# Batch 2's q and k by transposed loads, and six output tiles as half sums, in an attention and feed-forward kernel

## The chip, the cores and the metric

The kernel runs on one core of a Trainium2 chip. The metric is device microseconds of one execution. Before the change the median of three runs is 397.52 us (396.32 to 397.59). Engines are named as in the profile: PE (TensorE), with PEld for its weight loads, DVE (VectorE), ACT (ScalarE), POOL (GpSimd) and SP (SyncE, which here only issues DMAs).

## What is computed

```python
scale = 1.0 / np.sqrt(q.shape[-1])
scores = scale * np.matmul(q, k.transpose(0, 1, 3, 2))
m = np.max(scores, axis=-1, keepdims=True)
e = np.exp(scores - m)
attn = e / (np.sum(e, axis=-1, keepdims=True) + np.exp(-m) + 1e-09)
x = np.matmul(attn, v)                  # 8 batches, 12 heads, 448 tokens, 64 wide
x = x.transpose(0, 2, 1, 3).reshape(3584, 768)
h = x @ w_in                            # w_in 768 x 2048
g = np.maximum(h, 0.0) ** 2
out = g @ w_out                         # w_out 2048 x 768
```

Inputs and outputs are float32; the kernel computes in fp16 with float32 sums.

## The kernel before, in words

**Units.** A batch has 448 tokens and 12 heads; four heads are a *quad*, so a batch has three. Tokens are taken in seven chunks of 64. Scores come out transposed (keys on partitions): for one chunk of keys of a quad, PE writes a pair of PSUM banks (`sp`, two of these pairs) and ACT takes the exponential into fp16 (`exp`, line 245). The sum over keys is made by adding the chunks on DVE (`add_quad`) and by a matmul with ones; ACT makes the reciprocal as exp of minus ln; DVE multiplies it onto the values' product and so makes x (`quad_x`, line 478), transposed, which is what the in-projection wants. The in-projection (`half_in` for batch 0 in half-width tiles, `later_in` for the others) is followed by relu (ACT or DVE), a square on DVE into the ring `gs`, and the output product (`out_piece`, line 536), 384 columns of 128 tokens a tile, 16 blocks of 128 long in the sum. There are 56 such tiles.

**Shapes on PE.** The 128x128 array is used in three shapes. Scores, values and sums use four 64x64 quarters at once. The transposes of q and k use 128 rows by 64 columns. The in-projection of batches 0 and 1 and the first six output tiles use the full array. From batch 2 on (the cycles below) the in-projection runs as two column halves, and an output tile as four 64x64 products per block: the upper and the lower 64 rows of the sum go to two different PSUM banks, and two DVE or ACT instructions put them together (`out_first` scales the one bank into SBUF, `out_second` adds the other).

**How q and k are transposed.** `ON_PE` (line 37) names batches 0, 1 and 2: their q and k are loaded quad by quad with a cast to fp16 (`load_natural_quads`, POOL's queue), PE transposes chunk by chunk into PSUM (`transpose_one`, line 194: 14 matmuls for q or k of a quad), and DVE or ACT copies the result into `qk` (`transposed_copy`, line 201). Batches 3 to 7 go another way. `stage` (line 143, POOL's queue) copies q and k of a batch as fp16 into a buffer in DRAM; `transposed_loads` (line 160, SP's queue) reads it back with three transposing DMAs into `qk`: q, k, and k shifted by one token, since a row of 128 holds two tokens of 64. Even and odd keys then lie in different planes and halves, so a chunk of scores takes eight matmuls of 224 columns instead of four of 448 (`quad_scores`, line 391), and the last chunk's keys are put together by four copies on POOL (`tail_keys`, line 171).

**Order.** Nothing is scheduled by a program at run time: each engine works its own queue in the order in which the code emits. That order is written out in two strings. `ORDER` (line 662) holds everything up to 105.9 us: attention of batches 0 and 1 and most of 2, the in-projection of 0 and 1 and six output tiles. Its steps have one letter and numbers: `t`, `u`, `T`, `U` transposes and their copies, `s` and `e` a chunk of scores and its exponential (numbers up to 23 are batch 0 in half-width pieces; from 24 on seven to a quad), `p`, `b`, `y`, `z`, `n`, `x` values, sums, reciprocal and x of batch 0, `v`, `a`, `S`, `Z`, `M`, `X` the same for later quads, `i`, `r`, `g` and `j`, `k`, `l` in-projection, relu and square, `o`, `O` an output tile's product and its eviction, `d` a load out of the list `LOADS` (line 614). `CYCLE` (line 719) is then run for batches 3 to 7: attention of that batch, in-projection of the batch before, seven output tiles. Its only load step, `d0`, stands near its end and issues all that belongs to the next batch (`following`, line 693).

**Buffers.** Matmul results other than scores go through PSUM tiles `mp` (two banks at first, four from step `P0` on), reused in turn; `qk` has two buffers, output rows four (`ot`).

Of the kernel before, what the change touches and what calls it, by code (L numbers as in the profile page):

```python
# [16 lines left out]
def kernel(  # L17
# [19 lines left out]
    ON_PE = (0, 1, 2)  # L37
    COLS = H * S // 2 + 16
    HALF = DM // 2
# [119 lines left out]

    def transposed_loads(b):  # L160
        qk = qks[b] = qk_pool.tile([128, 3, COLS], FP16, name="qk")
        for i, n, x, c in ((0, "q", FRONT, H * S // 2), (1, "k", FRONT, H * S // 2), (2, "k", 0, COLS)):
            nc.sync.dma_start(
                out=qk[:, i, 0:c],
                in_=stages[n, b][x:x + c * 2 * D].rearrange("(r c) -> r c", c=2 * D),
                transpose=True,
            )
# [3 lines left out]
    def tail_keys(b):  # L171

        km = kms[b] = flat.tile([128, H, 64], FP16, name="flatq")
        for r in range(2):
            for odd in range(2):
                rows_ = slice(64 * r, 64 * r + 64)
                which, x = (1, 0) if odd == r else (2, odd)
                src = qks[b][rows_, which, x:x + H * S // 2].rearrange("p (h x) -> p h x", h=H)
                nc.gpsimd.tensor_copy(km[rows_].rearrange("p h (x o) -> p h x o", o=2)[:, :, :, odd],  # L179
                                      src[:, :, S // 2 - 32:S // 2])  # L180

    def qk_of(b):
        if b not in qks:
            qks[b] = qk_pool.tile([128, 3, COLS], FP16, name="qk")
        return qks[b]
# [203 lines left out]
    def quad_scores(m, c):  # L391
# [9 lines left out]
        if b in ON_PE:  # L401
            for i in range(2):
                for j in range(2):
                    r = slice(64 * j, 64 * j + 64)
                    x = (2 * g + i) * S
                    mm(sp[64 * i:64 * i + 64, j, 0:S], qk[r, 1, x + 64 * c:x + 64 * c + 64],
                       qk[r, 0, x:x + S], start=True, stop=True)
        else:
            n = S // 2
            for j in range(2):  # L410
                for i in range(2):
                    for o in range(2):
                        r = slice(64 * o, 64 * o + 64)
                        h = 2 * NQ * j + 2 * g + i
                        if c == KC - 1:
                            keys = kms[b][r, h, :]
                        else:
                            which, x = (1, h * n + c // 2) if c % 2 == o else (2, h * n + c // 2 + c % 2)
                            keys = qk[r, which, x:x + 190:3]
                        mm(sp[64 * i:64 * i + 64, o, j * n:(j + 1) * n], keys,  # L420
                           qk[r, 0, h * n:(h + 1) * n], start=True, stop=True)
# [178 lines left out]
    def load_quad(b, g):  # L600

        x = {(0, 1): (0, 0), (0, 2): (0, 1), (1, 0): (1, 0), (1, 1): (0, 0), (1, 2): (0, 1),
             (2, 0): (1, 0), (2, 1): (1, 1), (2, 2): (0, 0)}[b, g]
        if (b, x[0]) not in nats:
            nats[b, x[0]] = nat.tile([128, RUN * 2 * S], FP16, name=f"nn{x[0]}")
        load_natural_quads(b, (g,), x[1], nats[b, x[0]])

    def load_third():
# [5 lines left out]
    LOADS = ([lambda b=b, g=g: load_quad(b, g) for b in range(3) for g in range(NQ) if b + g]  # L614
             + [lambda b=b, g=g: load_v_quads(b, g, g + 1) for b in range(2) for g in range(NQ)]
# [3 lines left out]
             + [lambda: stage(3), load_third])  # L619

    def quad_visit(n):
# [32 lines left out]
        "o": lambda n, f0, f1: out_piece(128 * (n // 2), HALF * (n % 2), HALF, range(f0, f1)),  # L654
        "O": lambda n, act: out_done(128 * (n // 2), HALF * (n % 2), HALF, act),
    }

    def other_ring():
# [4 lines left out]
        d0 W8 c1,4,0 c0,0,1 c1,0,1 t0,0,0 c0,4,1 t1,0,0 u0,0,0,0 t1,0,4 u1,0,0,0 t0,0,4 u1,0,4,0 s0 d8 d1 u0,0,4,0 t0,1,0 e0 t1,1,0 u0,1,0,0 u1,1,0,0 s1 s2 e1  # L663
        d10 t0,1,4 u0,1,4,0 t1,1,4 u1,1,4,1 T0,1,0 T0,1,1 s3 U0,1,0,0,4,0 e2 U0,1,1,0,4,0 s4 U0,1,0,4,7,1 e3 d9 U0,1,1,4,7,0 d2 p0 e4 p2 s16 p1 e16 b0,0 b0,1
        p3 b0,2 b0,3 s6 y0 d18 s5 T0,2,0 e6 U0,2,0,0,4,0 z0 T0,2,1 U0,2,1,0,4,0 e5 U0,2,1,4,7,0 U0,2,0,4,7,0 s7 s9 b1,0 n0 b1,1 e7 x0 s8 p4 e9 b1,2 d3 b1,3 p5
        e8 p6 p7 s10 y1 b2,0 p8 p9 e10 s11 p10 b2,1 z1 e11 b2,2 b2,3 s12 p11 s13 n1 x1 y2 e12 T1,0,0 U1,0,0,0,7,0 T1,0,1 z2 n2 s14 e13 x2 p12 p13 s15
        U1,0,1,0,7,0 e14 e15 s17 p14 b3,0 b3,1 e17 s18 i0,7 d17 d5 b3,2 e18 b3,3 p15 y3 z3 b4,0 r0,7,0 s21 s19 e21 T1,1,1 d4 n3 b4,1 i0,6 U1,1,1,0,7,0 s20 d15
        T1,1,0 x3 b4,2 e19 b4,3 d16 s23 p16 p17 p18 r0,6,0 U1,1,0,0,7,0 e20 b5,0 e23 s22 e22 b5,1 p19 y4 s26 z4 n4 i0,4 g0,7 x4 r0,4,0 s27 i0,5 g0,6 b5,2 e26
        s25 e27 T1,2,1 s28 e25 p20 p21 r0,5,0 p22 s24 g0,5 b5,3 e28 d11 T1,2,0 p23 e24 s29 y5 e29 U1,2,1,0,7,0 U1,2,0,0,7,0 T2,0,0 T2,0,1 U2,0,0,0,7,0 z5 g0,4
        d6 U2,0,1,0,7,0 s30 n5 s32 a0,0 e30 d13 i0,0 i0,1 s33 x5 e32 r0,0,0 g0,0 r0,1,0 s31 i1,0 d12 g0,1 e33 i0,3 r1,0,0 e31 r0,3,1 s35 d7 s36 e35 P0 e36  # L670
        i0,2 s34 e34 a0,1 a0,2 g1,0 v0,0 a0,3 S0 v0,1 v0,2 v0,3 v0,4 Z0 v0,5 v0,6 M0 r0,2,0 g0,3 g0,2 s37 i1,3 a1,0 a1,1 e37 X0 r1,3,0 a1,2 g1,3 i1,6 s39 s40
        a1,3 e39 i1,1 r1,1,0 r1,6,0 s43 T2,2,0 e40 d20 T2,2,1 g1,6 e43 s42 g1,1 e42 U2,2,0,0,7,0 s41 d19 i1,5 r1,5,0 e41 s38 e38 T2,1,0 T2,1,1 U2,2,1,0,7,0
        U2,1,0,0,7,1 S1 a2,0 Z1 s44 U2,1,1,0,7,0 i1,4 i1,2 a2,1 e44 r1,4,1 s45 a2,2 g1,5 a2,3 v1,0 v1,1 M1 v1,2 v1,3 v1,4 v1,5 v1,6 r1,2,1 v2,0 S2 v2,1 X1
        g1,4 e45 g1,2 v2,2 v2,3 v2,4 Z2 v2,5 v2,6 M2 s47 X2 s46 i1,7 j3,0,2 r1,7,0 o0,0,4 j3,2,4 j1,0,2 j3,4,6 k3,0 j12,0,2 o0,4,8 j1,2,4 o0,8,12 e46 e47
        o0,12,16 s50 d21 g1,7 s51 j12,2,4 j1,4,6 k1,0 j5,0,2 e51 e50 l3 j5,2,4 j5,4,6 d23 O0,1 k5,1 j12,4,6 l5 o1,0,4 s48 s49 j6,0,2 e49 l1 e48 d22 k12,1 l12
        o1,4,8 o1,8,12 o1,12,16 s53 s52 e52 e53 j6,2,4 j10,0,2 o5,0,4 j6,4,6 O1,1 s55 k6,0 s54 j10,2,4 o5,4,8 j0,0,2 e55 a3,0 j10,4,6 j8,0,2 o5,8,12 j0,2,4
        a3,1 k10,1 o5,12,16 e54 s61 s57 l6 a4,0 j14,0,2 O5,0 e57 j14,2,4 j14,4,6 e61 j8,2,4 a3,2 j9,0,2 j9,2,4 j0,4,6 j9,4,6 a3,3 j8,4,6 l10 s56 k0,0 k14,0
        e56 l0 k8,1 s58 o2,0,4 o2,4,8 l14 d14 s59 v4,0 v4,1 v4,2 v4,3 a4,1 v4,4 v4,5 e58 k9,0 s60 e59 s64 o2,8,12 d24 l9 o2,12,16 a4,2 a4,3 j7,0,2 e60 v4,6
        e64 S4 Z4 M4 O2,0 S3 j7,2,4 o4,0,4 l8 o4,4,8 o4,8,12 o4,12,16 j7,4,6 Z3 s62 X4 s63 M3 O4,0 v3,0 v3,1 v3,2 v3,3 v3,4 v3,5 e62 v3,6 s65 X3 k7,1 j4,0,2
        e65 o3,0,4 a5,0 o3,4,8 o3,8,12 o3,12,16 j15,0,2 j4,2,4 j4,4,6 l7 e63 j15,2,4 a5,1 j2,0,2 O3,1 a5,2 j2,2,4 a5,3 j15,4,6 k4,0 j13,0,2 j11,0,2 S5 Z5  # L680
        k15,0 M5 l4 l15 j2,4,6 k2,0 j13,2,4 l2 j11,2,4 j13,4,6 j11,4,6 k11,1 k13,1 l11 l13
# [7 lines left out]
    def cycle(b):  # L689
# [3 lines left out]
        def following():  # L693
            if b + 1 < B:
                transposed_loads(b + 1)
                tail_keys(b + 1)
                load_v_quads(b + 1)
                if b + 2 < B:
                    stage(b + 2)
# [16 lines left out]
            "d": lambda n: following(),  # L716
# [7 lines left out]
        v1,2 v1,3 M1 v1,4 O5,0 v1,5 Q5 v1,6 X1 o6,0,2 s3,4 e3,4 o6,2,4 s3,0 e3,0 o6,4,6 o6,6,8 a2,0 o6,8,10 o6,10,12 s3,1 o4,0,2 o6,12,14 a2,1 s3,3  # L724
        e3,1 o4,2,4 o6,14,16 s3,2 e3,3 o4,4,6 O6,1 a2,2 o4,6,8 s3,5 a2,3 o4,8,10 Q6 o4,10,12 e3,2 e3,5 o4,12,14 o4,14,16 O4,1 Q4 a3,0 s3,6 v2,0 v2,1
        S2 Z2 v2,2 v2,3 v2,4 v2,5 M2 v2,6 e3,6 X2 j2,0,2 j2,2,4 j2,4,6 k2,0 j13,0,2 j13,2,4 l2 j13,4,6 j3,0,2 k13,1 l13 j3,2,4 j15,0,2 j12,0,2 j15,2,4
        j0,0,2 j3,4,6 a3,1 j15,4,6 k3,1 a3,2 k15,1 j12,2,4 a3,3 l15 j0,2,4 j0,4,6 l3 j12,4,6 j10,0,2 j10,2,4 j4,0,2 k0,0 l0 k12,1 l12 j10,4,6 j6,0,2
        j7,0,2 j7,2,4 j7,4,6 j4,2,4 k10,0 j6,2,4 j4,4,6 l10 j6,4,6 k7,1 j5,0,2 l7 j5,2,4 k4,1 j11,0,2 k6,0 j11,2,4 j11,4,6 j9,0,2 l6 j5,4,6 l4 j9,2,4
        j8,0,2 j8,2,4 k5,1 j9,4,6 l5 j1,0,2 k11,0 j8,4,6 j1,2,4 j1,4,6 k9,1 j14,0,2 j14,2,4 l11 l9 k8,0 j14,4,6 l8 k1,1 l1 k14,0 S3 Z3 d0 l14 M3
# [61 lines left out]
```

## Time and profile before

The profile is of one execution, which took 396.87 us in all; its span from first to last instruction is 394.8 us.

| | before |
|---|---|
| median of 3 runs | 397.52 us |
| profiled execution | 396.87 us |
| its span | 394.8 us |
| PE / DVE / ACT / POOL busy | 385.5 / 240.5 / 238.1 / 59.8 us |
| granted PE clock | 1.00 throughout |
| first step of the first cycle (values) starts | 105.9 us |
| bytes moved by DMA | 45.33 MB |

How to read it: an engine's busy time is the union of its instructions' times. PE's matmuls are pipelined, so its busy time includes the tails of matmuls that overlap the next; what a step costs PE is read from when the next one starts. "64*64 64x384" is a matmul on a 64x64 part of the array with 384 columns out. In the chain of waits each piece is the work that the end waited for at that time; "x28" counts instructions. "Idle before" with "issue" is time in which an engine waited for nothing that the trace shows. In rows of DMA queues the share is of 16 engines; it passes 100% since an engine has several packets under way.

### The profile page before, as it was taken

The numbers are of one execution on the slowest core, as the hardware profiler recorded it, in microseconds if no ns is written. First come the engines' busy times: TensorE is split into PE (matmuls) and PEld (weight loads), VectorE is DVE, ScalarE is ACT, GpSimd is POOL, SyncE is SP. The second block draws the span as 40 slices with busy tenths as digits, with TensorE's granted clock in tenths as the row PEclk, the third lists the DMA queues.
The fourth block names the chain that finished last, engine by engine and source line by source line (L and its number), as shares of the span: only waits on it lengthen the run. The fifth ranks groups of instructions, "written<-read, shape, count | busy, mean of one in ns | idle before, by whom it ended". The sixth has DMA issues, their size and how long they took to land.

```text
span 394.8 us, 13877 instructions
## 1 busy us (share of the span) xinstructions
PE 385.5 (98%) x6252; PEld 262.9 (67%) x6252; DVE 240.5 (61%) x445; ACT 238.1 (60%) x324; POOL 59.8 (15%) x96
## 2 busy tenths in 40 slices
PE   8789999999999999999999999999999999999997
PEld 4567776445599766896579866776677765555665
DVE  3889994385746765668536876567646785285000
ACT  4999895768479625895279834896269934100111
POOL 8354500003200032000500016000500000000000
PEclk9999999999999999999999999999999999999999
DMA  8999999568942579419692398527652100100222
GB/s 146 203 204 206 203 206 208 98 127 154 191 85 63 113 140 181 96 43 161 113 203 75 77 193 127 129 64 141 126 74 68 58 7 2 62 0 14 68 80 81
DMA packets 75051, 45.33 MB, mean 115 GB/s; under 512 B 47472, under 2 KB 72944, under 8 KB 74992
## 3 DMA queue, kind: packets, MB, share of 16 engines
q0 software_dynamic: 24752, 22.62, 36.3%
q1 hardware_dynamic: 49952, 21.59, 25.0%
q8 instruction: 49, 0.80, 0.8%
q10 hardware_dynamic: 288, 0.23, 0.2%
q14 instruction: 10, 0.08, 0.1%
HBM read 45.69 MB, written 17.93 MB: 161 GB/s over the span
## 4 chain that ended last, share of the span: by engine, by line
PE 94%; DVE 3%; ACT 1%; issue 1%; DVEq 0%; ACTq 0%
PE mp L92 81%; PE sp L92 9%; PE xp L92 2%; PE mp L198 2%; ACT et L245 1%; DVE qk L208 1%; DVE half L334 1%; DVE half L332 0%; PE mp L225 0%; ACT rcp L356 0%; ACT rcp L363 0%; DVE qk L235 0%; DVE half L338 0%; DVE half L336 0%; DVE rt L496 0%
## 5 line engine op out<-in xcount | busy, mean ns | idle before, releaser
L92 PE MATMUL mp<-wout,gs 64*64 64x384 f16 (+2 forms) x2592 | 166.7, 322 | 0.0
L92 PE MATMUL mp<-xt,win 128*64 128x448 f16 (+2 forms) x1344 | 151.4, 339 | 0.1
L245 ACT ACTIVATE et<-sp 128x896 f16<-128x896 f32 (+1 forms) x131 | 110.8, 889 | 30.1 <-PE sp L92 28.9
L92 PEld LDWEIGHTS <-win 128*64 128x64 f16 (+1 forms) x1344 | 89.6, 106 | 58.7 <-issue 7.4
L92 PEld LDWEIGHTS <-gs 64*64 64x64 f16 (+1 forms) x2592 | 105.9, 106 | 34.3 <-issue 1.1
L494 ACT ACTIVATE rt<-mp 128x448 f16<-128x448 f32 x55 | 29.3, 544 | 57.2 <-PE mp L92 52.4
L500 DVE TENSOR_TENSOR gs<-rt 128x448 f16<-128x448 f16 x128 | 49.2, 401 | 22.2 <-ACT rt L494 19.8
L92 PE MATMUL sp<-qk 64*64 64x224 f16 (+1 forms) x1056 | 57.4, 274 | 2.5 <-issue 0.9
L496 DVE TENSOR_SCALAR rt<-mp 128x448 f16<-128x448 f32 x73 | 45.2, 621 | 23.0 <-PE mp L92 21.5
L557 ACT ACTIVATE ot<-mp 128x384 f32<-128x384 f32 (+2 forms) x34 | 16.4, 481 | 51.3 <-PE mp L92 50.8
L92 PEld LDWEIGHTS <-qk 64*64 64x64 f16 x1056 | 36.1, 114 | 14.4 <-issue 7.4
L179 POOL COPY flatq<-qk 64x384 f16<-64x384 f16 x20 | 12.4, 643 | 205.9 <-DMA qk<-stage_k 205.6
L245 ACT ACTIVATE nn<-sp 128x896 f16<-128x896 f32 x42 | 36.7, 915 | 1.9 <-PE sp L92 1.8
L478 DVE TENSOR_TENSOR xt<-mp,rcp 128x448 f16<-128x448 f32 x42 | 24.3, 620 | 20.0 <-ACT rcp L457 17.8
L92 PEld LDWEIGHTS <-vn 64*64 64x64 f16 x756 | 24.1, 107 | 9.8 <-issue 2.6
L563 DVE SCALAR_TENSOR_TENSOR ot<-mp,ot 128x384 f32<-128x384 f32 x35 | 19.5, 556 | 16.9 <-ACT ot L557 15.3
L454 ACT ACTIVATE rcp<-sp,one_b 128x896 f32<-128x896 f32 x21 | 21.2, 1007 | 10.0 <-PE sp L92 10.0
L92 PE MATMUL mp<-et,vn 64*64 64x448 f16 (+1 forms) x448 | 25.1, 343 | 0.0
L559 DVE TENSOR_SCALAR ot<-mp 128x384 f32<-128x384 f32 x23 | 12.8, 556 | 19.6 <-PE mp L92 19.5
L432 DVE TENSOR_TENSOR half<-et 128x1792 f16<-128x1792 f16 x15 | 16.3, 1087 | 7.0 <-ACT et L245 6.9
L457 ACT ACTIVATE rcp<-rcp 128x896 f32<-128x896 f32 x21 | 20.0, 952 | 0.6
L434 DVE TENSOR_TENSOR half<-half,et 128x1792 f16<-128x1792 f16 x15 | 16.4, 1091 | 0.7 <-ACT et L245 0.3
(59 smaller groups left out, 198.2 us busy)
## 6 DMA issues: line engine op xcount, KB each, us to landing
out_dram<-ot SPq DMA_DIRECT2D x52, 96.0 KB, 2.3
out_dram<-ot SPq DMA_DIRECT2D x19, 192.0 KB, 1.9
win<-in_moe_w_in_dram POOLq DMA_DIRECT2D x8, 384.0 KB, 11.1
wout<-in_moe_w_out_dram POOLq DMA_DIRECT2D x4, 768.0 KB, 15.6
vn<-in_v_dram POOLq DMA_DIRECT2D x10, 288.0 KB, 4.8
stage_q<-in_q_dram POOLq DMA_DIRECT2D x4, 676.0 KB, 8.8
stage_k<-in_k_dram POOLq DMA_DIRECT2D x4, 676.0 KB, 12.0
nn<-in_q_dram POOLq DMA_DIRECT2D x8, 224.0 KB, 8.1
```

The costliest lines, as they stand in the source:

```text
L92: return nc.tensor.matmul(out_, lhsT, rhs, start=start, stop=stop)
L245: nc.scalar.activation(out=out_, in_=in_, func=AF.Exp, scale=scale)
L432: nc.vector.tensor_add(esq[m], a[:, 0:w], a[:, w:2 * w])
L434: nc.vector.tensor_add(esq[m], esq[m], z[:, 0:w])
L454: nc.scalar.activation(out=rcp, in_=zp[:, :, 0:S], func=AF.Ln, bias=one_b)
L457: nc.scalar.activation(out=zqs[m], in_=zqs[m], func=AF.Exp, scale=-1.0)
L478: nc.vector.tensor_mul(xts[b][:, 2 * g + i, :], xqs[m][i][:, 0:S], zqs[m][:, i, :])
L494: nc.scalar.activation(out=rt[:, 0:m], in_=hp[:, 0:m], func=AF.Relu)
L496: nc.vector.tensor_scalar(out=rt[:, 0:m], in0=hp[:, 0:m], scalar1=0.0, scalar2=None, op0=ALU.max)
L500: nc.vector.tensor_mul(gs[:, f0:f0 + per, t0 % RING:t0 % RING + n], r, r)
L557: nc.scalar.activation(out=ot, in_=op[:, 0:w], func=AF.Copy, scale=OUT_SCALE)
L563: nc.vector.scalar_tensor_tensor(out=ot, in0=lo[:, 0:w], scalar=OUT_SCALE, in1=ot, op0=ALU.mult, op1=ALU.add)
```

## The change

Batch 2 leaves `ON_PE`. Its q and k are staged in DRAM as those of the later batches are, but read back quad by quad: for each of the two head pairs of a quad three small transposing loads (448, 448 and 464 rows), 18 in all, on SP's queue. A pair's shifted keys take 464 columns (`WIDE`), so their place in `qk` is reckoned anew (`odd_keys`). The last chunk's keys are put together quad by quad, by four smaller POOL copies each. The `T` and `U` steps of batch 2 go, and so do its natural loads; two copies for staging come. v of batch 2 is loaded in four parts, in the order of keys that the later batches have, and its output rows are stored in that order.

The six output tiles of `ORDER` are computed as four 64x64 products per block, with two evictions (`O` and the new step `Q`) and two PSUM banks each.

`ORDER` is rewritten throughout. In the cycles the one step `d0` becomes seven: the three transposed loads of the next batch (`d0 d1 d2`) stand after the fifth stored tile, the key copies, the staging and v (`d3 d4 d6 d5`) after the seventh.

```diff
-    ON_PE = (0, 1, 2)
+    ON_PE = (0, 1)
     COLS = H * S // 2 + 16
+    PAIR, WIDE = S, S + 16
+    BY_QUADS = 2
...
+    def transposed_quad(b, g):
+        qk = qk_of(b)
+        for j in range(2):
+            p = g + NQ * j
+            for i, (n, x, w) in enumerate((("q", FRONT, PAIR), ("k", FRONT, PAIR), ("k", 0, WIDE))):
+                x += p * PAIR * 2 * D
+                nc.sync.dma_start(
+                    out=qk[:, i, p * w:(p + 1) * w],
+                    in_=stages[n, b][x:x + w * 2 * D].rearrange("(r c) -> r c", c=2 * D),
+                    transpose=True,
+                )
...
+    def tail_keys_of_quad(b, g):
+
+        if b not in kms:
+            kms[b] = flat.tile([128, H, 64], FP16, name="flatq")
+        dst = kms[b].rearrange("p (j g i) (x o) -> p j g i x o", j=2, g=NQ, o=2)
+        for which, w in ((1, PAIR), (2, WIDE)):
+            pairs = qks[b][:, which, 0:H // 2 * w].rearrange("p (j g c) -> p j g c", j=2, g=NQ)
+            for r in range(2):
+                rows_ = slice(64 * r, 64 * r + 64)
+                odd, x = (r, 0) if which == 1 else (1 - r, 1 - r)
+                src = pairs[rows_, :, g, x:x + S].rearrange("p j (i x) -> p j i x", i=2)
+                nc.gpsimd.tensor_copy(dst[rows_, :, g, :, :, odd], src[:, :, :, S // 2 - 32:S // 2])
+
+    def odd_keys(b, h):
+        return h // 2 * WIDE + h % 2 * (S // 2) if b == BY_QUADS else h * (S // 2)
...
-                            which, x = (1, h * n + c // 2) if c % 2 == o else (2, h * n + c // 2 + c % 2)
+                            which, x = (1, h * n + c // 2) if c % 2 == o else (2, odd_keys(b, h) + c // 2 + c % 2)
...
-    LOADS = ([lambda b=b, g=g: load_quad(b, g) for b in range(3) for g in range(NQ) if b + g]
-             + [lambda b=b, g=g: load_v_quads(b, g, g + 1) for b in range(2) for g in range(NQ)]
+    LOADS = ([lambda b=b, g=g: load_quad(b, g) for b in ON_PE for g in range(NQ) if b + g]
+             + [lambda: stage(BY_QUADS)]
+             + [lambda b=b, g=g: load_v_quads(b, g, g + 1) for b in ON_PE for g in range(NQ)]
...
-             + [lambda: stage(3), load_third])
+             + [lambda: stage(3), load_third]
+             + [lambda f=f, g=g: f(BY_QUADS, g) for g in range(NQ) for f in (transposed_quad, tail_keys_of_quad)])
...
-        "o": lambda n, f0, f1: out_piece(128 * (n // 2), HALF * (n % 2), HALF, range(f0, f1)),
-        "O": lambda n, act: out_done(128 * (n // 2), HALF * (n % 2), HALF, act),
+        "o": lambda n, f0, f1: out_piece(128 * (n // 2), HALF * (n % 2), HALF, range(f0, f1), True),
+        "O": lambda n, act: out_first(128 * (n // 2), HALF * (n % 2), HALF, act),
+        "Q": lambda n: out_second(128 * (n // 2), HALF * (n % 2), HALF),
...
-        def following():
+        def following(n):
             if b + 1 < B:
-                transposed_loads(b + 1)
-                tail_keys(b + 1)
-                load_v_quads(b + 1)
-                if b + 2 < B:
+                if n < 3:
+                    transposed_load(b + 1, n)
+                elif n < 5:
+                    tail_keys(b + 1, (n - 2,))
+                elif n == 5:
+                    load_v_quads(b + 1)
+                elif b + 2 < B:
                     stage(b + 2)
```

In the new `ORDER` the staging of batch 2 is `d5`; the loads of its quads 1, 0 and 2 are `d25`, `d23` and `d27`, their key copies `d26`, `d24` and `d28`. The first scores of batch 2 are `s54` (quad 1):

```diff
+        x5 i0,5 e25 d5 e29 i1,6 d18 g0,4 g0,7 s30 r0,5,0 a0,0 e30 s33 d25 a0,1 r1,6,1 i1,7 s32 i1,2 g1,6 e33 g0,5 e32 r1,2,1 r1,7,0 P0 a0,2 s34 s35
...
+        v1,5 v1,6 S2 r1,4,1 v2,0 v2,1 v2,2 M1 X1 v2,3 v2,4 v2,5 v2,6 s54 Z2 s56 j1,0,2 j7,0,2 M2 j1,2,4 e56 e54 X2 j7,2,4 j1,4,6 j7,4,6 j12,0,2
+        j12,2,4 g1,1 g1,4 k7,1 j12,4,6 d27 k1,0 l7 s55 o2,0,4 s57 k12,0 e55 e57 d26 o3,0,4 d12 o3,4,8 s52 o2,4,8 s58 d21 o2,8,12 l1 e52 e58 s53 l12
```

## The prediction

> **What bounds the kernel now.** I read the busy shares first, then the chain of work that ended last, then busy time by stage.
>
> ```profile
> PE 385.5 (98%) x6252; PEld 262.9 (67%) x6252; DVE 240.5 (61%) x445; ACT 238.1 (60%) x324; POOL 59.8 (15%) x96
> PE 94%; DVE 3%; ACT 1%; issue 1%; DVEq 0%; ACTq 0%
> ```
>
> TensorE (PE) is busy 98% of the span and is 94% of the chain. So time goes only where PE has less to do, changes its shape of work less often, or waits less. The stages say where it waits (columns: window, its length, then busy time of PE, PEld, DVE, ACT, POOL, then clock, DMA share, GB/s):
>
> ```profile
> 10.00:20.00 10.00, 7.16 (x216) 5.30 (x215) 8.28 (x20) 10.00 (x18) 3.43 (x6) 1.00 1.26 204
> 20.00:30.00 10.00, 8.71 (x216) 6.88 (x212) 8.51 (x18) 9.60 (x15) 6.00 (x9) 1.00 1.25 203
> 30.00:40.00 10.00, 9.82 (x183) 7.67 (x172) 9.10 (x20) 9.67 (x14) 4.37 (x7) 1.00 1.25 206
> ```
>
> Up to about 40 us ACT is full and PE waits; DMA moves some 204 GB/s all the while. After that PE is full, and I read its prices from the chain (start, us, what):
>
> ```profile
> 51.66 0.90 PE mp L198 x28
> 68.13 0.50 PE sp L92 x8
> 121.47 0.38 PE sp L92 x16
> 112.46 0.97 PE mp L92 x24
> ```
>
> L198 is the transposes: 0.90 us per quad for q and k of batch 2. Two score chunks cost 0.50 us as 8 matmuls between full 128x128 work, 0.38 as 16 half-wide matmuls between 64x64 work. So the keys' other form costs nothing on PE, and going into the full shape costs 0.12. Coming back costs another 0.11 (the 0.65 us steps of line 536 last 0.74 when a score follows, and the first full step is 0.01 longer). A round trip between shapes is 0.23 us.
>
> Output blocks are last. In the timeline 16 full matmuls begin at 92.02 and the next work at 94.62: 2.60 us a tile. The 24 small matmuls of 0.97 us above are six blocks, 0.162 each, so 16 blocks are again 2.60 us.
>
> ```profile
> 92.02 2.76 PE L92 MATMUL mp<-wout,gs 128*128 128x384 f16 x16
> 94.62 0.54 PE L92 MATMUL mp<-xt,win 128*128 128x448 f16 x2
> ```
>
> **The change, part by part,** against the profiled execution (396.87 us: span 394.8 and 2.07 around it; it lies 0.65 under the median 397.52, and I add nothing for that).
>
> *Transposes off PE.* Six groups of 14 matmuls go. Without shape changes a group is 0.39 us (0.90 for two, less 0.12 for the way in): **-2.33**. Their six evictions (0.62 us on DVE, one 0.80 on ACT) go too; PE is the bound there, so no gain.
>
> *Fewer shape changes.* In the written order PE changes shape 66 times before and 53 times after: between 64x64 and full 42, now 33; between 64x64 and the transposes' 128x64, 22, now 18. 13 changes at half of 0.23 is **-1.50**. The six tiles themselves are 2.60 us each in both forms: 0. Their second eviction (six of 0.56 us on DVE) lies beside full PE stages in which DVE is about half idle (22.6 of 36 us busy from 70 to 106); price 0, and if a PSUM bank came late, under 1 us each. The shortest turnaround of a bank in the new order is 1.1 us of PE work against a 0.62 us eviction; in the old one it was 1.3, with no wait. I keep 0.4 in all for such small waits: **+0.4**.
>
> *The start.* From ACT's exponential of the third score group (9.62) to the last reciprocal of batch 0 (ends 38.51) the old order has 22 full exponentials at 0.80, the new one 20, but also a copy (0.80) and a relu (0.43), and it can begin 0.17 earlier: 0.5 us less. The last x of batch 0 would be done about 38.6, or 37.6 if ACT's own short waits (0.9 us in all) went. PE work ahead of the first tile that needs that x, summed at the prices above from the end of the warm-up at 4.3 us: 31.5 before, where PE really began it at 40.75 (9.3 behind), 29.0 after, so 8.6 to 9.7 behind: -0.7 to +0.4, and I take **0**.
>
> *Batch 2 by copies and transposed loads.* PE issues nothing for it, so it costs only if late. The staging copies stand on POOL's queue behind 7.4 MB of other loads and are 1.38 MB; with the first quad's 0.45 MB that is 9.2 MB, of which 1.47 land by 10 us (147 GB/s) and the rest at 204: about 48 us. Then SP issues six loads for quad 1. The nearest rows are the large ones, six times as long:
>
> ```profile
> 83.60 2.40 SPq L163 DMA_TRANSPOSE qk<-stage_q  x1
> 86.10 5.88 SPq L163 DMA_TRANSPOSE qk<-stage_k  x2
> q1 hardware_dynamic: 7912, 2.17, 93.9%
> ```
>
> 2.76 us each, while in that window (82 to 93 us) their queue kept the 16 engines 93.9% busy. So the large load is bound by its data, and a small one should be a sixth: 0.46. Its ends are 0.46 and 2.76; I take 0.46, for that reason. Sharing the engines equally with the loads behind it doubles this; then quad 1 is there at 48 + 6 x 0.92 + 3.2 (a large load lands 5.9 after issue, 3.2 after the issue ends) = 57 us. Its first score has 53.0 us of PE work ahead and 9.3 of lag: 62.3. Five microseconds to spare: **0**. Queued behind: on SP the first output stores (four output buffers, so no one waits yet), on POOL, behind quad 1's four key copies (at most 0.64 us each, the row of the larger ones), v of batch 2 and the staging of batch 3, both wanted 15 us later or more.
>
> *The cycle.* Batch b+1's transposed loads go ahead of two stores, and v and staging from about 147-160 us (the next cycle's output stage) into the in-projection stage, some 7 us earlier. Two stores then wait about 8 us on SP; their buffers are wanted again 20 us later. What can be won:
>
> ```profile
> 161.28 0.26 PE L92 MATMUL sp<-qk 64*64 64x224 f16 x1
> 162.41 0.40 PE L92 MATMUL sp<-qk 64*64 64x224 f16 x7 [0.88 <-issue]
> ```
>
> PE stops inside a group of scores whose operands are there, 1.09 us more than the group needs. Nothing shown releases it; DMA had been at 213 GB/s until just before. The table of queues has 49 packets of 16 KB of kind instruction, which is one per 255 of PE's 12,506 instructions, and they share those engines. In the output stage PE uses its instructions over twice as fast as in the in-projection. I read it as late instructions, and with the traffic moved it goes: **-1.09**; bounds 0 and -1.09. The Trainium skill ("Runtime: NRT & Kernel Launch", Instruction fetch mechanics) says that instructions stream in 16 KiB blocks of 256 and that crossing a block is mostly hidden; the packets agree in size. By that rule the stop has another cause and stays, and the sum would be 393.4.
>
> Sum: 396.87 - 2.33 - 1.50 + 0.4 + 0 - 1.09 = **392.4**.
>
> **Rivals.**
>
> *Quad 1 late by sharing.* From 40 to 58 us the load queue is never empty:
>
> ```profile
> q0 software_dynamic: 4594, 3.63, 128.7%
> stage_k<-in_k_dram POOLq DMA_DIRECT2D x1, 676.0 KB, 21.3
> ```
>
> 4594 packets in 18 us on 16 engines is one per 63 ns and engine. A quad is 2720 rows of 256 bytes, 170 per engine, at 21 ns (7912 in 11 us at 93.9%). If packets take turns one by one, each waits for a large one: about 84 ns. The five loads that wait for k's copy (142 rows an engine) then need 12 us: 48.5 + 12 + 1 to 3 = 61.5 to 63.5, up to 1.2 late. If they get nothing until the 2.8 MB behind the copies are through (about 62), 67.5: 5 late. So 392.4 to 397.4, middle 394.9. For it: the output store lands in 2.7 us at 62-72 us, in 2.2 when the queue is empty. Against: equal sharing gives 5 us to spare. The Trainium skill ("DMA: Bandwidth & Descriptors", Queues, rings and completion order) states the turn by packets; by it alone the time would be 392.4 to 393.6. No run here shows the two kinds together.
>
> *Slower: a fixed price per small load.* If a load of a sixth costs SP what a large one does (c = 2.76), quad 1 is there at 48.5 + 5c + 3.2 = 65.5, 3.2 late, and quad 2 at 48.5 + 17c + 3.2 = 98.6 where its first score, so delayed, comes at 90.5: 8.1 late. Together 17c - 35.6 = 11.3, so **403.7**. It decides from c = 2.43 on (5.7 us lost, 398.1). For it: only large loads were seen. Against: they are data-bound.
>
> *The start eats it.* Less PE work stands ahead of the last x (29.0 for 31.5), so PE could simply wait more: with 2 us more lag, 394.4, with 4, 396.4.
>
> *It does not do what it says:* PE gets its 3.8 us, and waits on ACT or DVE take it back: 396 to 397. Against: from 60 to 100 us neither is busy for over 80% of any ten.
>
> **Chances.** Forecast (391 to 394) 0.62; quad 1 late by more than 1.5 us 0.17; start 0.07; taken back 0.04; fixed price 0.10. Over 0.3% (1.2 us, about what a measurement of this kernel can tell from no change) faster: 0.62, nearly all of the second and third, 0.82 in all; within it 0.07; slower 0.11, mostly the fixed price. The range runs from the best start and no small waits (391.3, with the runs' own spread 390.8) to the late quad's and the start's upper part, 396.6; it leaves out the fixed price and some tails.
>
> **What would show it.** Transposes of batch 2 gone and PE's busy time near 382; two score chunks after the first 60 us at 0.38; no wait of PE ahead of the first score of batch 2 near 62 us, and a small transposed load issued in about half a microsecond (over 2 would make me wrong, to the slow side); PE at the first tile that needs the last x of batch 0 at 38 to 39 us; cycles all of 45.2 us, without the stop. Wrong I would be above all by a PE wait at that first score, or by PE lagging over 11 us at 40 us.

## The result, and the profile after

The changed kernel takes 403.19 us (median of four runs, 403.02 to 403.52) beside 397.14 us (396.32 to 397.59) of the kernel before on the same chip. The ratio is 1.0156, with a 95% interval of 1.0135 to 1.0176: 1.6% slower, where 392.4 us and a range up to 396.6 were forecast. Here and below a median is of all runs, and a ratio leaves out the slow ones, those over 1.5% above the fastest of the same kernel. Its profiled execution took 403.52 us with a span of 401.7, so 6.65 us more than the profiled execution before.

From the page of the changed kernel: the busy times, the granted clock of PE in 40 slices of 10 us, and the chain of work that ended last by engine.

```profile
PE 384.4 (96%) x6540; PEld 261.0 (65%) x6540; DVE 238.5 (59%) x439; ACT 240.7 (60%) x330; POOL 63.7 (16%) x107
PEclk9999997799999999999999999999999999999999
PE 73%; DMA 13%; SPq 8%; POOL 2%; DVE 1%; issue 1%; ACT 0%; POOLq 0%; ACTq 0%
```

PE is still busy for 96% of the span, but it is 73% of the chain instead of 94%: transfers and the engine that issues them (SPq) hold 21%. Two slices of the clock are not full, the seventh and the eighth, 60 to 80 us. The busy time by stage (columns as in the prediction) says what happens there:

```profile
20.00:30.00 10.00, 9.20 (x222) 7.30 (x211) 8.94 (x20) 9.97 (x17) 3.73 (x6) 1.00 1.24 206
30.00:40.00 10.00, 10.00 (x137) 7.53 (x134) 7.96 (x16) 9.30 (x15) 4.42 (x6) 1.00 1.26 205
60.00:70.00 10.00, 1.68 (x33) 0.83 (x21) 2.67 (x6) 1.85 (x2) 0.65 (x2) 0.76 1.37 161
70.00:80.00 10.00, 9.88 (x125) 5.38 (x129) 2.24 (x5) 4.64 (x6) 4.37 (x8) 0.73 1.31 183
```

From 20 to 40 us PE is busier than before (9.20 and 10.00 for 8.71 and 9.82): the start became shorter. From 60 to 70 us PE works for 1.68 us of ten. The timeline of PE shows the wait and its releaser:

```profile
61.00 0.29 PE L94 MATMUL sp<-qk 64*64 64x224 f16 x4
67.32 0.39 PE L94 MATMUL sp<-qk 64*64 64x224 f16 x1 [6.03 <-DMA qk<-stage_k]
70.12 0.78 PE L94 MATMUL sp<-qk 64*64 64x224 f16 x11 [2.40 <-DMA qk<-stage_k]
```

The first scores of batch 2 (`s54`) begin at 61.0 us, a little ahead of the forecast 62.3. Four of their matmuls have their operands, the rest wait for the transposed loads of quad 1: 8.4 us.

The stages laid end to end give the account of the loss. The first cycle begins at 113.56 us instead of 105.91, 7.65 later. The first four cycles take 45.60, 45.17, 45.17 and 45.17 us instead of 45.23, 46.34, 45.34 and 45.17, 0.97 less together. What follows is 0.2 longer. So all of the loss lies ahead of 113.6 us.

### The profile page after: what moved, and what is told of

Its sections match the earlier page's. It is cut to its first block, busy times and chain, and to the rows that moved or that the text cites. A ratio compares the mean times of both kernels' runs of the same rounds, so it can differ in the third digit from the quotient of the medians.

```text
span 401.7 us, 14494 instructions
## 1 busy us (share of the span) xinstructions
PE 384.4 (96%) x6540; PEld 261.0 (65%) x6540; DVE 238.5 (59%) x439; ACT 240.7 (60%) x330; POOL 63.7 (16%) x107
## 3 DMA queue, kind: packets, MB, share of 16 engines
q0 software_dynamic: 24384, 22.63, 36.8%
## 4 chain that ended last, share of the span: by engine, by line
PE 73%; DMA 13%; SPq 8%; POOL 2%; DVE 1%; issue 1%; ACT 0%; POOLq 0%; ACTq 0%
PE mp L94 67%; SPq L179 8%; PE sp L94 7%; DMA stage_k<-in_k_dram 4%; DMA win<-in_moe_w_in_dram 4%; DMA qk<-stage_k 2%; DMA nn<-in_k_dram 2%; POOL nn L118 1%; POOL flatq L217 1%; POOL vn L106 1%; DVE gs L538 0%; SPq L569 0%; DVE half L472 0%; ACT ot L595 0%; DVE xt L516 0%
## 5 line engine op out<-in xcount | busy, mean ns | idle before, releaser
L94 PEld LDWEIGHTS <-win 128*64 128x64 f16 (+1 forms) x1344 | 90.6, 107 | 60.3 <-issue 8.8
L283 ACT ACTIVATE et<-sp 128x896 f16<-128x896 f32 (+2 forms) x131 | 110.8, 892 | 29.5 <-PE sp L94 28.9
L94 PEld LDWEIGHTS <-gs 64*64 64x64 f16 (+1 forms) x2880 | 103.7, 106 | 31.8 <-issue 0.4
L532 ACT ACTIVATE rt<-mp 128x448 f16<-128x448 f32 x61 | 32.7, 544 | 65.9 <-PE mp L94 54.0
L534 DVE TENSOR_SCALAR rt<-mp 128x448 f16<-128x448 f32 x67 | 41.6, 621 | 27.9 <-PE mp L94 26.3
L201 POOL COPY flatq<-qk 64x384 f16<-64x384 f16 x20 | 13.9, 693 | 152.8 <-DMA qk<-stage_k 152.3
L283 ACT ACTIVATE nn<-sp 128x896 f16<-128x896 f32 x42 | 36.7, 915 | 2.1 <-PE sp L94 2.1
L601 DVE SCALAR_TENSOR_TENSOR ot<-mp,ot 128x384 f32<-128x384 f32 x41 | 22.8, 555 | 19.2 <-ACT ot L595 15.6
L94 PEld LDWEIGHTS <-vn 64*64 64x64 f16 x756 | 22.9, 107 | 9.5 <-issue 1.1
```

The source lines that it names most:

```text
L94: return nc.tensor.matmul(out_, lhsT, rhs, start=start, stop=stop)
L283: nc.scalar.activation(out=out_, in_=in_, func=AF.Exp, scale=scale)
L532: nc.scalar.activation(out=rt[:, 0:m], in_=hp[:, 0:m], func=AF.Relu)
L534: nc.vector.tensor_scalar(out=rt[:, 0:m], in0=hp[:, 0:m], scalar1=0.0, scalar2=None, op0=ALU.max)
L601: nc.vector.scalar_tensor_tensor(out=ot, in0=lo[:, 0:w], scalar=OUT_SCALE, in1=ot, op0=ALU.mult, op1=ALU.add)
```

## The experiments

Theory: the PE time was won as forecast, but quad 1's small transposed loads take turns with the load queue packet by packet and land near 70 us, and the wait halves PE's clock for some time after it. Rivals: the new form of the work is dear in itself (the loads, the order or the half-sum tiles), so that nothing is won by having q and k in time; or the DMA engines are so full that every transfer put ahead makes another late. Each row below stands beside runs of the kernel before on its own chip (396.03 to 396.69 us).

| kernel | median, us | ratio, 95% interval |
|---|---|---|
| changed, run again | 402.51 | 1.0132 (1.0098 to 1.0166) |
| fill | 403.67 | 1.0150 (1.0093 to 1.0207) |
| hold | 403.66 | 1.0171 (1.0125 to 1.0218) |
| early | 405.64 | 1.0215 (1.0189 to 1.0240) |
| narrow | 405.27 | 1.0218 (1.0183 to 1.0252) |
| hold, second | 400.03 | 1.0070 (1.0047 to 1.0093) |
| late | 396.67 | 1.0021 (0.9992 to 1.0050) |
| full tiles | 396.87 | 1.0015 (1.0002 to 1.0028) |
| late, second | 395.99 | 0.9989 (0.9968 to 1.0009) |
| late, third | 395.33 | 0.9967 (0.9950 to 0.9984) |
| cycle alone, on the kernel before | 395.29 | 0.9967 (0.9952 to 0.9982) |

### Once more: the changed kernel itself

> The changed kernel itself, on the chip of the other three, as their reference. Theory: 403 us, the wait at the first scores of batch 2 ends when quad 1 lands, near 70 us, and the clock is halved for about 10 us from 65. Rival (the late landing was an accident of one profile): quad 1 lands before 62 in this profile and the time is 392 to 396.

It came again: `s54` began at 61.22 us, its last operands came at about 70, and the clock fell again (402.51 us). The late landing is no accident of one profile.

### Hold: the second half of wout behind quad 1

```diff
-    ... v0,6 a1,0 d19 r1,3,1 ... a1,2 d20 g1,3 ...      (second half of w_out: d19, d20)
+    ... e57 d26 d19 d20 ...                             (behind quad 1's key copies; tiles 3 and 4 change places)
```

> The changed kernel with the two loads of the second half of w_out (1.57 MB) issued behind quad 1's key copies instead of ahead of them, and with output tiles 3 and 4 exchanged in the order so that these columns are wanted later. Theory (quad 1's small loads take turns, packet by packet, with the loads queued behind the staging copies): only 1.2 MB is left to share with, it is through at about 59 us, the rest of quad 1 then comes at some 900 packets a us, and it is there at 62 to 63 us: a wait of 1 to 2 us instead of 9, no half clock, 391 to 393 us. Rival (the small loads are slow by themselves, or late only because the staging lands late): the wait stays at 8 to 9 us and the time at 402 to 404 us.

Busy engines by queue, 55 to 60 us, first of the changed kernel, then of this one (packets, MB, time of the packets as a share of 16 engines):

```profile
q0 software_dynamic: 797, 0.62, 90.8%
q1 hardware_dynamic: 796, 0.20, 43.5%
```

```profile
q1 hardware_dynamic: 2177, 0.52, 136.8%
q0 software_dynamic: 112, 0.09, 10.9%
```

With both queues full, 797 load packets and 796 packets of the transposing queue go through: one for one, though a load packet moves 768 or 896 bytes and a transposing one 256. With the load queue nearly empty the transposing queue moves 2.7 times as many. Up to there nothing but the other queue changed, so this is the sharing. Its PE timeline:

```profile
61.21 0.55 PE L94 MATMUL sp<-qk 64*64 64x224 f16 x16
70.10 0.27 PE L94 MATMUL sp<-qk 64*64 64x224 f16 x4
76.11 0.40 PE L94 MATMUL sp<-qk 64*64 64x224 f16 x4 [5.74 <-DMA qk<-stage_k]
```

Quad 1 is now in time, with no wait at 61.2. But the held loads meet quad 0's: the same wait, 5.7 us, stands one quad later, and another of 2.3 us follows. The theory of the cause holds; the expected gain of some 11 us does not come (403.66; the profile is of the fastest of the four, 400.52), and the second rival gains weight.

### Narrow: load packets of half the size

```diff
-        nc.gpsimd.dma_start(out=wout[:, i * w:(i + 1) * w, n0:n0 + HALF], in_=wout_r[:, i * w:(i + 1) * w, n0:n0 + HALF])
+        for c in (n0, n0 + HALF // 2) if n0 else (n0,):
+            m = HALF // 2 if n0 else HALF
+            nc.gpsimd.dma_start(out=wout[:, i * w:(i + 1) * w, c:c + m], in_=wout_r[:, i * w:(i + 1) * w, c:c + m])
```

> The changed kernel with the second half of wout loaded in column halves: twice as many packets of 384 instead of 768 bytes, the same bytes. If the transposing queue and the load queue take turns packet by packet, a transposing packet now waits for a shorter one: quad 1 lands near 66 us instead of 70, the wait of 9 us shrinks to about 5, 398 to 400. Rival (the two queues share the engines by time or bytes): quad 1 lands near 70 as before, or later by the price of small packets, 403 to 405.

Its queues from 60 to 65 us, and then PE:

```profile
q0 software_dynamic: 1103, 0.42, 87.6%
q1 hardware_dynamic: 1099, 0.27, 67.5%
```

```profile
64.25 0.30 PE L94 MATMUL sp<-qk 64*64 64x224 f16 x1 [1.88 <-DMA qk<-stage_k]
65.77 0.50 PE L94 MATMUL sp<-qk 64*64 64x224 f16 x11 [1.22 <-DMA qk<-stage_k]
```

Again one for one, 1103 to 1099, with load packets of 384 bytes, and quad 1 comes at 65.8 us instead of 70.1. Sharing by time or by bytes would not have moved it. The Trainium skill ("DMA: Bandwidth & Descriptors", Queues, rings and completion order) states a turn by packets, a packet there being several descriptors. The counts agree with a turn; how many of the profile's packets one turn holds no run here shows. The time, 405.27 us, missed what was expected: the small packets carry fewer bytes in all (0.69 MB for 0.90 in those 5 us), so what stands behind them is later (quad 0 by 4.4 us, in the table below), and PE waits 6.6 us until 98.4 us for quad 0's key copies, which stand behind quad 2's on POOL.

### Early: staging ahead of the in-projection's weights

```diff
-    ... b2,3 d15 d9 d14 d4 d17 ... i0,5 e25 d5 e29 ...
+    ... b2,3 d15 d5 d9 d14 d4 d17 ... i0,5 e25 e29 ...
```

> The changed kernel with the staging copies of batch 2 issued after the third quarter of w_in, 2.3 MB of loads earlier. Theory (late staging and turns by packet together): staging lands at about 39 us, quad 1 shares with the other loads at about 180 packets a us and is there at 55 to 58 us, ahead of its first use at 61, so no wait there and no half clock; the other loads are put back by the staging and by the sharing, some 4 to 6 us, so that the first output tile may wait up to 3 us for w_out: 391 to 395 us. If only the staging's place counted and sharing cost the others nothing: 390.5 us. If the small loads' own pace were to blame and needed 25 us or more: a wait of some us stays at 61, 395 us or more.

Quad 1's loads were issued from 37.5 us instead of 46.9, their last packet went through at 57.7, and PE did not wait at 61: that much came as the theory says. But w_in, now behind 1.38 MB of staging, held PE for 5.8 us at 41 us, and the wait for quad 0's key copies grew to 7.0 us, in a profile of an execution of 411 us (so the sizes are rough). It is the second rival: what is put ahead makes the next transfer late.

### Fill: PE kept busy through the wait

```diff
-    ... v2,5 v2,6 s54 Z2 s56 ...
+    ... v2,5 v2,6 f46 s54 Z2 s56 ...       (46 matmuls of constants, results unused)
```

> The changed kernel with 46 dummy matmuls of 448 columns (8.6 us at full clock) in front of the first scores of batch 2; nothing is left out. Theory: the clock of PE falls to half because PE idles while it waits for quad 1's q and k. Then the wait itself stays (PE goes on at about 70 us), the clock stays at 1.00 and the 2.7 us lost at half clock come back: 400.5 us. Rival: the clock falls for another reason (the amount of traffic, or the time since the start): 403.2 us, and 10 us at half clock as before.

In the profiled execution (400.85 us) the fill ended at 70.26, when quad 1 was there. Compare the same 18 matmuls of the in-projection, of the changed kernel and of this one:

```profile
70.82 5.84 PE L94 MATMUL mp<-xt,win 128*128 128x448 f16 x18
```

```profile
70.78 3.58 PE L94 MATMUL mp<-xt,win 128*128 128x448 f16 x18
```

That is 2.26 us for the half clock, read directly; with the scores ahead of them it is about 2.6. The runs agree only in part: two took 400.7 and 400.9 us, as expected, and two 406.5 and 408.3, of which there is no trace. Their mean granted clock was 0.990 and 0.991, which at half speed is some 8 us (an estimate: 1% of 405 us, doubled), so in those two the clock fell after all, and the record does not say where. So the price of the half clock rests on these rows, not on the median.

### Late: other work ahead of batch 2's scores

```diff
-    v2,6 s54 Z2 s56 j1,0,2 j7,0,2 M2 ... j12,4,6 d27 ... s55 o2,0,4 s57 ... O2,0 s46 o3,8,12 Q2 s48 ... j9,0,2 ... d28 ... d24
+    v2,6 Z2 j1,0,2 j7,0,2 M2 ... j12,4,6 d27 ... j9,0,2 ... j4,4,6 s54 s56 ... o2,0,4 s55 ... o3,12,16 ... d24 d21 d28 j14,0,2 ... s46 s48
```

> The changed kernel with four more in-projection tiles of batch 1 (9, 10, 11, 4; 4.5 us of PE) ahead of the first scores of batch 2, quad 1's scores beside the output tiles 2 and 3, quad 0's first scores behind those, and on POOL the key copies of quad 0 ahead of those of quad 2 and the staging of batch 3 between them. Theory (the loss is q and k that come late, and the half clock that follows a long wait): the first scores of batch 2 stand at about 69.4 us, quad 1 lands near 70, so the 9 us wait shrinks to about 1, the clock stays at 1.0, and 403.2 becomes 392 to 395. Rival (the DMA engines are full up to 93 us, so what quad 1 no longer waits for, quads 0 and 2 do): PE waits 3 to 6 us at the first scores of quad 0 or 2 instead, 396 to 400.

All instructions, loads and bytes of the change are still there, and 396.67 us is 1.5% under the changed kernel's 402.51 us: the new form of the work is not dear in itself. The run makes three moves at once (the later scores, the order of the key copies, the place of batch 3's staging), and what each is worth alone it does not show. In its profile, of an execution of 400.02 us and so 3.3 over the median, the clock stayed at 1.00 there, `s54` stood at 69.56 us and waited 0.4. The largest of PE's waits from 60 to 125 us:

```profile
PE mp L94 <- issue: 2.5, 2, 1.3
PE sp L94 <- DMA qk<-stage_k: 1.3, 4, 0.5
PE mp L94 <- ACT rt L532: 0.7, 1, 0.7
```

### Hold, second: held loads and later scores of quad 0

```diff
-    ... o2,12,16 O2,0 s46 o4,8,12 Q2 s48 o4,12,16 e46 s50 j9,0,2 ... d28 ... d24 ... e48 ... e50       (from the kernel "hold")
+    ... o2,12,16 O2,0 o4,8,12 Q2 o4,12,16 j9,0,2 ... d24 d21 d28 ... j4,4,6 s46 s48 ... e46 ... e48 ... j0,4,6 s50 e50
```

> The kernel that holds the second half of wout back behind quad 1's key copies, with quad 0's first scores moved behind seven pieces of in-projection tiles more (from 70.1 to about 76 us), quad 0's key copies ahead of quad 2's on POOL and the staging of batch 3 between them. Theory: quad 1 in time at 61 us as in the kernel that held wout back, quad 0 (landed at 76.1 there) now in time too, quad 2 near 85 where it is wanted at 88: no wait over 1 us, clock 1.0, 391 to 394. Rival (DMA engines full): quad 2 late by 3 us or more, 395 to 399.

400.03 us, 0.7% slower than the kernel before. Its profile is of an execution of 408 us, with PE waiting 4.6 us for v of batch 2 at 84 us and 5.2 us for q and k; how much of that its median runs had, no trace shows. The rival had the side right; the time is over its 399.

### Late, second, and late, third: one chain of transfers

```diff
 late, second:
-    ... s54 s56 e54 e56 k4,1 ... Q3 a4,0 d24 d21 d28 j14,0,2 a4,1 ...
+    ... s54 s56 k4,1 e54 e56 ... Q3 a4,0 d24 d28 d21 j14,0,2 a4,1 a4,2 a4,3 ...
 late, third, besides:
-    ... d23 a1,1 ... j12,4,6 d27 ...
+    ... d23 d27 a1,1 ... j12,4,6 ...
```

> The kernel with the later first scores of batch 2, and three moves in queues: the staging of batch 3 on POOL behind the key copies of all quads of batch 2 instead of between them; on ACT the relu of tile 4 ahead of the first exponential of batch 2; on DVE quad 1's sum over keys in one go. Theory (quad 2 is late there because each of its packets shares the engines with the staging of batch 3): quad 2 is through by about 84 us instead of 92, the waits at its first scores (0.9 us) and the one of 0.7 us for the relu go, 394.5 to 395.8. Rival (the DMA engines are full, so what comes later is late itself): batch 3's staging, issued some 8 us later, makes PE wait at the first scores of the first cycle, 397 to 399.

> The kernel with the later first scores of batch 2 and the three moves in queues, and one move more: quad 2's six transposed loads stand on SP directly behind quad 0's, ahead of the first output stores. In the kernel without this move the transposing queue stood empty from 72.0 to 76.3 us, quad 2 was through at 83.1, the staging of batch 3 was issued at 85.0, and PE waited 1.65 us at 106.2 for batch 3's keys; the first cycle took 49.1 us, the later ones 45.2. Theory (from 50 to 106 us the time is set by one chain of transfers, and what comes earlier in it ends earlier): quad 2 is through by 80, batch 3's keys are there some 3 us earlier, the wait of 1.65 us goes, 393.6 to 395.2. Rival (the wait is for PE's other inputs too, or the late stores cost as much): 395.7 to 396.7, no change.

The packet records of the trace say when the last transposing packet of each quad went through:

```
us                quad 1   quad 0   quad 2   first cycle begins, takes
changed           67.8     72.4     93.3     113.56, 45.60
narrow            65.1     76.8     95.6     117.91, 45.16
hold              59.9     75.3     91.2     111.11, 45.17
late              67.5     72.4     92.0     107.84, 47.37
late, second      67.8     71.8     83.1     103.10, 49.08
late, third       68.1     72.5     82.4     102.83, 47.49
before            -        -        -        105.91, 45.23
```

With batch 3's staging out of its way quad 2 is through 9 us earlier than in the first late version, whose profile is of a long execution; beside the full tiles below (87.3 us), which have the staging in the same place as that version, it is 4 us. The first cycle begins 2.8 and 3.1 us ahead of the kernel before. But the second version gives it back there: the cycle takes 3.9 us more than the later ones, of which 1.65 us is the wait for batch 3's keys. The rival was right on the place and wrong on the time (395.99 us). In the third version that wait is a third, and the time is 395.33 us, 0.3% under the kernel before, just over the 395.2 expected (quad 2 is through at 82.4, not by 80). Between the second and the third version the intervals of the ratios overlap. Of the 2.3 us that the third version's first cycle takes over its later ones, these two lines of its PE timeline hold 1.1; another stop with "issue", of 0.42 us, follows at 123.8:

```profile
104.86 0.40 PE L94 MATMUL sp<-qk 64*64 64x224 f16 x8 [0.54 <-DMA qk<-stage_k]
118.17 0.35 PE L94 MATMUL mp<-wout,gs 64*64 64x384 f16 x1 [0.59 <-issue]
```

### Full tiles: the six early tiles back in the full shape

```diff
-        "o": lambda n, f0, f1: out_piece(128 * (n // 2), HALF * (n % 2), HALF, range(f0, f1), True),
+        "o": lambda n, f0, f1: out_piece(128 * (n // 2), HALF * (n % 2), HALF, range(f0, f1)),
```

(on the kernel "late"; `O` evicts the whole tile, the `Q` steps go)

> The kernel with the later first scores of batch 2, and its six early output tiles back in the full 128x128 shape with one eviction each. The written order then changes PE's shape 91 times instead of 55, since these tiles stand between scores. Theory (a change costs half of 0.23 us): 36 changes, 4.1 us more than with half sums, 400 to 401.5. Rival (changes cost nothing and tiles are 2.60 us in either form): within 0.5 us of it, 396 to 397.

396.87 us, no 4 us more, though PE's price was about as the theory said. In the written order PE goes into the full shape 35 times and out of it 36. A chunk of scores between two output pieces takes 0.32 to 0.34 us there for 0.19 among 64x64 work, and four full blocks ahead of scores 0.75 for 0.65, so a round trip is 0.23 to 0.25 us, and PE is busy for 387.0 us. The second late version, run beside it on the same chip and with half sums, has 383.5 (the first one, which differs in the tiles alone, has no profile near its median). But PE waits less in return:

```profile
PE sp L94 <- issue: 0.5, 1, 0.5
PE sp L94 <- DVE half L476: 0.4, 1, 0.4
PE mp L94 <- DVE xt L516: 0.2, 1, 0.2
```

It no longer waits for a transfer between 60 and 125 us. Its first cycle begins at 105.99 us, 2.9 later than in the second late version, and takes 46.03 us, 3.1 less. So in this stretch PE's work alone no longer sets the end: less of it is made up by longer waits. From 60 to 125 us the second late version waits 3.0 us more, 1.65 of it for batch 3's keys and most of the rest with "issue". That transfers set the end is shown for the first part; for the rest it is not.

### The cycle alone, on the kernel before

```diff
-    ... j14,4,6 l8 k1,1 l1 k14,0 S3 Z3 d0 l14 M3                                   (all loads of the next batch)
+    ... O5,0 v1,5 Q5 d0 d1 d2 v1,6 ... O4,1 Q4 d3 d4 d6 d5 a3,0 ...                (transposed loads; keys, staging, v)
```

> The kernel before with the new place of the loads in the cycles alone (transposed loads after the fifth stored tile, key copies, staging and v after the seventh). Theory (the stop of 1.09 us at 161 us comes of instructions that are fetched late behind the staging and v loads): the stop is gone and nothing else moves: 1.0 to 1.1 us less than the kernel before, 396.0 us. Rival (the stop has another cause): no difference beyond 0.3 us, or the stop is in its profile again.

395.29 us, 1.4 us less than the kernel before (interval 0.7 to 1.9), and the cycle with the stop took 45.17 us instead of 46.34. This small part of the change is as fast as the best version of all of it, and both are faster than either kernel.

## Why the prediction was wrong, point by point

The account of the 7.65 us that are lost ahead of the first cycle, by what PE's steps took over their steady prices: `s54` 8.94, `s56` 0.51 and the six in-projection pieces behind it 2.19 (half clock), the tile and scores at 94.7 to 97 us 1.40, together 13.0. So 5.4 us were won, and the terms of the sum are 2.33 for the transposes, 1.50 for the shapes and what the start gave, 1.6: 5.4.

**Transposes off PE and fewer shape changes: right in size.** 0.23 to 0.25 us a round trip between shapes was measured, 0.23 forecast; the 2.33 us of the transposes fit the sum and were not measured alone. In the third late version, which has 55 changes for the 66 of before, 2.33 + 1.2 + 1.6 less the 1.6 us of its small waits gives 3.5, and its first cycle begins 3.1 us ahead. The full tiles show that such time need not count where transfers and stops lie beside it.

**The start: forecast 0, measured -1.6, beyond the bound of -0.7.** The last x of batch 0 was done at 36.8 us, where 37.6 to 38.6 was forecast, and PE began the tile that needs it at 36.7, 7.7 us behind its work instead of 9.3.

**Batch 2 in time: this step failed.** "... then quad 1 is there at 48 + 6 x 0.92 + 3.2 (...) = 57 us. ... Five microseconds to spare: **0**." It was there at 70. Taken apart on the changed kernel's own rows:

```profile
46.91 1.21 SPq L179 DMA_TRANSPOSE qk<-stage_q  x1
50.09 2.44 SPq L179 DMA_TRANSPOSE qk<-stage_k  x2
52.57 1.27 SPq L179 DMA_TRANSPOSE qk<-stage_q  x1
53.89 4.83 SPq L179 DMA_TRANSPOSE qk<-stage_k  x2
```

k's staging was there at 50.1 us, 2 later than reckoned. The first transposing packet went at 50.8, 3.9 us after the first issue. The 2720 packets of quad 1 then took 17.1 us, 101 ns a packet and engine, since each waited for a load packet; the forecast had 5.5 us in all (0.92 a load), and the rival "late by sharing" 84 ns for five of the six loads. The last landing came 2.3 us after the last packet (50.8 + 17.1 + 2.3 = 70.2). Sharing "equally" was taken as equal time, and it is equal packets. The rival "late by sharing" had the mechanism and 0.17 of the chance, and was short in size: by turns alone it had 61.5 to 63.5 us, with a start at 48.5 and 12 us of packets for the 50.8 and 17.1 measured. Its worst case, 67.5, came from another thought, that the loads get nothing until the load queue is through, and was short too. Equal packets were also in a sentence that the prediction cited from the Trainium skill ("DMA: Bandwidth & Descriptors", Queues, rings and completion order), and they were set aside for equal sharing with five microseconds to spare.

**What no step counted: the clock.** After the long wait PE came back at half speed. In the changed kernel, by stage:

```profile
64.50:65.50 1.00, 0.00 (x0) 0.00 (x0) 0.00 (x0) 0.00 (x0) 0.00 (x0) 0.85 1.74 47
65.50:75.00 9.50, 5.28 (x24) 2.24 (x25) 0.22 (x1) 1.73 (x2) 5.02 (x10) 0.50 1.25 159
```

The granted clock is 0.50 from 65.2 to 75.4 us. It begins 3.9 us after PE's last matmul ended and outlasts the wait by 5.3 us. The Trainium skill ("TensorE: Matmul & The Clock Gate", Part 1) says that PE falls back to half rate after an idle window of about 3.4 us; this trace agrees. Other runs show that PE need not be idle for so long: in "narrow" waits of 1.88 and 1.22 us drew 3.4 us of half clock, and one of 1.89 us did in the changed kernel run again. So a wait can cost more than its length: behind the 8.4 us of waiting about 2.6 us more were lost at half clock.

**A second wait, not forecast.** `s51` needs quad 0's key copies (L217), and these stood on POOL behind quad 2's, which waited for transposed loads until 93.8 us:

```profile
93.84 2.95 POOL L217 COPY flatq<-qk 64x128 f16<-64x128 f16 x8 [19.29 <-DMA qk<-stage_k]
96.46 0.77 PE L94 MATMUL sp<-qk,flatq 64*64 64x224 f16 x8 [0.90 <-POOL flatq L217]
```

The prediction named what stands behind quad 1's copies, and not that `d28` was written ahead of `d24`.

**The cycle: right.** -1.09 was forecast; the stop is gone in the changed kernel, and alone the new place is worth 1.4 us (0.7 to 1.9).

**The fixed price per load: rightly set aside.** Quad 1's first four small loads took some 1.2 us each to issue, so c was between the ends 0.46 and 2.76, under the 2.43 from which it decides; the last two took 2.4 each (4.83 for both), when the queue's packets were already going at 101 ns. Half a microsecond, the sign that the prediction named, was not seen. The time came near that rival's 403.7 by another cause, which is luck.

Whether the sum holds where no transfer is late is not shown. The third late version took 395.07 us in its profiled execution, and with a first cycle like its others (45.17 us for 47.49) that would be 392.75; no kernel here reached it, and of those 2.3 us only 0.54 is a wait for a transfer. That it lies near 392.4 is in part two misses that cancel: the start gave more than forecast, and small waits took 1.6 us for 0.4.

**What stays open.** Why two runs of the fill took 6 us more, and where their clock fell. What the moves in the first late version are worth one by one. And whether an order exists in which all of the saving comes through: three reorders moved it from 402.5 to 395.3 us.

## What to carry to other kernels

Work taken off the bounding engine and given to DMA is free only where the DMA engines have room at that time: sum the packets of all queues in the stage, not the bytes, and give each packet of a small transfer the time of one of the large transfer beside it. A wait of some microseconds on PE is priced at its length and the half clock that may follow it: 8.4 us drew 2.6 more here, and one of 1.9 us drew some too. And a queue's order decides who waits behind whom: copies that wait for a late load belong behind those whose data is there.

## What the runs showed of the hardware

Two DMA queues that are both full share the engines packet for packet, whatever their sizes: beside 256-byte transposing packets, 797 to 796 with load packets of 768 and 896 bytes and 1103 to 1099 with 384 bytes, each in 5 us, and 219 to 217 from 80 to 84 us in the changed kernel with the 3328-byte ones of the staging copies. A transposing packet so took 101 ns an engine beside the first and 295 beside the last (4 us x 16 engines / 217). From 85 to 90 us, with the load queue at 23.6% of the engines' time for 95.6% before, it was 673 to 80: that queue was no longer full. A transposing packet's record lasts 18 ns with the other queue empty, 31 ns with it full.

The granted clock of PE goes in steps: all 14 stretches at half clock in these traces, but for those at the very end, lasted 3.41, 6.83 or 10.24 us. Laid on steps of 3.41 us, the step ahead of each fall had PE busy for 0 to 54% of its time, so PE was not always idle there: in "hold" at 18.4 us it was several stops, the longest of them 0.69 us. From the rows alone the border lies near half: steps 44 to 54% busy were followed by a fall in some cases and not in others.

PE's stops with "issue" as their cause end a fixed time after a packet of kind instruction: in eleven such stops in six kernels (the kernel before, the changed one's fill, the late ones and the full tiles) PE went on 1.2 to 1.6 us after the end of the last such packet. So I read them as late instructions, which no run here shows apart. They came mostly in half-sum tiles, where PE uses four times as many instructions for the same work, and in seven of the eleven the DMA engines' busy share was over 100% in the 3 us before. The Trainium skill ("Runtime: NRT & Kernel Launch", Instruction fetch mechanics) calls this crossing mostly hidden; here most of the 49 to 51 packets of a run passed without a stop, and these eleven did not.
